# First MoE products alone, the second chunk behind them, the second tile's keys behind two weight blocks

## The chip, the core and the metric

One core of a Trainium2 chip runs the whole program. TensorE (PE) multiplies, VectorE (DVE), ScalarE (ACT) and GpSimd (POOL) compute beside it, SyncE (SP) issues most transfers. The metric is the device time of one execution in microseconds (us). TensorE's clock is granted at one of two levels, 1.2 or 2.4 GHz; the profile gives it as a share of the upper one (PEclk).

## The reference

A delta-rule attention feeds two layers of experts:

```python
k_n = k / (np.linalg.norm(k, axis=-1, keepdims=True) + 1e-06)
for t in range(S):                       # q, k, v: (4, 8, 768, 48)
    y[:, :, t] = einsum('bhd,bhde->bhe', q[:, :, t], state)
    v_old = einsum('bhde,bhd->bhe', state, k_n[:, :, t])
    state = state + beta[..., t] * outer(k_n[:, :, t], v[:, :, t] - v_old)
...
x = y as (3072 tokens, 384)
h = x @ w_in                             # 384 -> 2048
x = (h * sigmoid(1.702 * h)) @ w_out     # 2048 -> 384: "MoE 1"
p = domain_probs / (domain_probs.sum(-1, keepdims=True) + 1e-09)
out = sum over e < 4 of p[:, e] * (relu(x @ w1[e]) @ w2[e])   # 384 -> 1024 -> 384: "MoE 2"
```

## The kernel before

**Attention by chunks.** The 768 steps are cut into 12 chunks u of 64 steps; all 32 (batch, head) pairs of a chunk are computed together, in two halves of 16. Two chunks make a *tile* of 512 tokens (6 tiles). A chunk needs its keys scaled and turned (`queue_keys`, `queue_turn`: L364 load, L374 square, L377 sum, L389 to L407 inverse root by Newton steps, L420 scaling, L338 transposition, L344 copies into `kt`), Gram products of the keys (`queue_g`, L516 and L519; evicted by L524 and copies to `g`), masked products of keys and queries (`queue_q`, L447, masked by L452 into `pq`), and a triangular inverse. The first tile's inverse is VectorE's (`queue_first_inverse`): two blocks of 16 in parallel, a multiplication by beta (L626), a transposition to rows (L590), then joining products on TensorE, L656 and L665, each for both chunks. Later tiles' inverses run on GpSimd in 30 pairs of steps (`queue_inverse`, L567 and L569), begin with a transposition on VectorE (L558) and end with L573 and L590.

**The chain.** `queue_chain` carries the state SU from chunk to chunk: keys times state (L728), subtraction from v (L731), solve (L738), cross product (L748), subtraction (L753), second solve, reading of y (L761), writing of the state (L766), addition to SU (L780, L783). The copies of y go through `stage` by transfers (L842), and are split into high and low halves `xs` (`split_x`, L872), the MoE's input.

**MoE 1.** w_in and w_out are cut into 16 blocks f. A product in full precision takes three passes over high and low halves. For a block, nine products of layer 1 (L878, into `ph`) are followed by the gate on ScalarE (L979, L981), its low half `gh` on VectorE (L982), and nine products of layer 2 (L964). Layer 2 of a block stands one block later. Tile 0 runs blocks 0 to 7 on 256 columns (chunk 0) and then on the other 256 (chunk 1), blocks 8 to 15 on 512; tile 1 runs all blocks in halves (`HALVED`).

**Weight blocks.** They come as 64-bit numbers (`queue_w1`): a load (L252), scaling on ScalarE (L261), three integer instructions on VectorE (L264, L268, L272), the high half on ScalarE (L277), the low half (L280) on GpSimd or VectorE.

**The order.** All instructions of attention and weights are tasks of an `Order`: a planner with one clock per engine, a cost for each task, dependencies and a priority. It writes each engine's queue at build time; on the chip each engine works its queue in order and waits at semaphores. Between two MoE products `tick` lets it put in tasks; a task of TensorE only when `due` has run down:

```python
    def run(self, pe_ok):
        while True:
            t = self.pick(self.now, pe_ok or self.due <= 0)
            if t is None:
                return
            if t.pe:
                self.due = PE_SHARE * t.engs["PE"]
            t.issue()
```

`until(*ts)` issues tasks until those named are planned as done. Before the MoE it waits for chunk 0's y and block 0:

```python
        queue_tile(1)
        until(ydone[0], wdone[0])
```

## Time and profile before

| | us |
|---|---|
| median of 3 runs (lowest, highest) | 1516.05 (1513.36, 1517.55) |
| the profiled execution | 1515.38 |
| its span, first to last instruction | 1513.7 |
| PE busy | 1434.6 (95%) |
| DVE, ACT, POOL busy | 645.0, 460.0, 216.0 |
| mean granted clock of TensorE | 0.962 |

The attention's preparation takes the first 87 us. From there MoE 1 runs to some 700 us with attention put in, then MoE 2 to the end. "Busy" of PE is not speed: the clock column tells at which level it worked. Where PE is idle the timeline gives the gap and the engine that ended it; "issue" means that the profile shows no cause.

### The profile page before, as it was taken

What the parts mean: (1) busy time and instruction counts of PE and PEld (TensorE: products, weight loads), DVE (VectorE), ACT (ScalarE), POOL (GpSimd) and SP (SyncE); (2) the same over time, 40 slices, a digit from 0 to 9 for tenths busy, and PEclk for the clock granted to TensorE, in tenths of its full rate; (3) what the DMA queues carried; (4) which work ended last, traced back from release to release, by engine and by line L of the source; (5) the groups of instructions that cost most, each with busy time, mean ns of one, the idle gap of its engine ahead of it and who ended that gap; (6) DMA issues with size and microseconds to landing.
All of it is one profiled execution on the core that took longest, in us unless ns stands there. A gap on an engine that the chain in (4) does not pass through costs nothing.

```text
span 1513.7 us, 30460 instructions
## 1 busy us (share of the span) xinstructions
PE 1434.6 (95%) x13552; PEld 1270.2 (84%) x13552; DVE 645.0 (43%) x1076; ACT 460.0 (30%) x869; POOL 216.0 (14%) x351
## 2 busy tenths in 40 slices
PE   2689879998999999999999999999999999999998
PEld 2579669997888888887999999999999999999998
DVE  6868766647537433332223243222342223423222
ACT  5436343434334333342112131111221112212111
POOL 3214902860081170000000000000000000000000
PEclk8559979999999999999999999999999999999999
DMA  9211012012201100230000020000110000100001
GB/s 341 81 36 27 1 42 52 2 36 71 58 1 43 30 22 15 81 112 0 1 0 1 1 73 11 0 1 0 43 42 1 0 1 11 53 21 22 21 22 42
DMA packets 41333, 53.72 MB, mean 35 GB/s; under 512 B 25713, under 2 KB 29937, under 8 KB 41201
## 3 DMA queue, kind: packets, MB, share of 16 engines
q1 hardware_dynamic: 41008, 51.67, 11.1%
q8 instruction: 106, 1.74, 0.5%
q14 instruction: 27, 0.21, 0.0%
q10 hardware_dynamic: 192, 0.10, 0.0%
HBM read 42.71 MB, written 7.86 MB: 33 GB/s over the span
## 4 chain that ended last, share of the span: by engine, by line
PE 75%; DMA 1%; DVE 1%; issue 0%; SPq 0%; ACT 0%; DVEq 0%; ACTq 0%
PE ph L878 35%; PE po L1077 26%; PE px L964 8%; PE ch L738 1%; PE ch L728 1%; PE y L761 1%; PE gp L447 1%; DMA raw<-in_we_dram 1%; PE ch L766 1%; PE ch L748 1%; PE gp L516 0%; DMA stage<-scr 0%; DVE xs L872 0%; SPq L1053 0%; DVE oacc L1085 0%
## 5 line engine op out<-in xcount | busy, mean ns | idle before, releaser
L878 PE MATMUL ph<-xs,w 128*128 128x512 f32 (+1 forms) x2808 | 667.7, 381 | 3.8 <-DVE x L178 2.4
L878 PEld LDWEIGHTS ph<-xs,w 128*128 128x128 f32 x2808 | 503.0, 191 | 91.4 <-issue 2.8
L1077 PE MATMUL po<-w,hh 128*128 128x384 f32 x2304 | 432.8, 336 | 0.0
L1077 PEld LDWEIGHTS po<-w,hh 128*128 128x128 f32 x2304 | 407.6, 188 | 17.1
L1104 DVE SCALAR_TENSOR_TENSOR hh<-ph,hh 128x512 fp32r<-128x512 f32 x192 | 132.8, 692 | 555.8 <-ACT hh L1103 555.8
L1103 ACT ACTIVATE hh<-ph 128x512 fp32r<-128x512 f32 x192 | 114.8, 598 | 634.1 <-PE ph L878 634.1
L964 PE MATMUL px<-gh,w 128*128 128x512 f32 (+1 forms) x1080 | 235.9, 357 | 4.9 <-DVE gh L982 4.8
L964 PEld LDWEIGHTS px<-gh,w 128*128 128x128 f32 x1080 | 178.8, 192 | 35.6 <-DVE gh L982 7.6
L982 DVE TENSOR_TENSOR gh<-ph,gh 128x512 fp32r<-128x512 f32 (+1 forms) x120 | 69.5, 580 | 154.4 <-ACT gh L981 153.4
L979 ACT ACTIVATE ph<-ph 128x512 f32<-128x512 f32 (+1 forms) x120 | 59.5, 496 | 214.6 <-PE ph L878 211.5
L569 POOL TENSOR_TENSOR scr<-scr,itmp 128x30 f32<-128x30 f32 (+9 forms) x150 | 91.0, 607 | 11.8
L567 POOL TENSOR_TENSOR itmp<-scr 128x30 f32<-128x30 f32 (+9 forms) x150 | 82.0, 547 | 11.4
L981 ACT CAST gh<-ph 128x512 fp32r<-128x512 f32 (+1 forms) x120 | 60.1, 501 | 3.8
L738 PEld LDWEIGHTS ch<-v,scr 32*32 32x32 f32 x1536 | 41.3, 119 | 21.3 <-issue 16.2
L738 PE MATMUL ch<-v,scr 32*32 32x48 f32 x1536 | 45.7, 220 | 13.6 <-issue 10.4
L178 ACT COPY su<-ch 32x384 f32<-32x384 f32 x81 | 38.0, 470 | 52.6 <-PE ch L738 47.4
L516 PE MATMUL gp<-kt 48*32 48x64 f32 x768 | 29.9, 238 | 20.1 <-ACT kt L344 19.8
L516 PEld LDWEIGHTS gp<-kt 48*32 48x32 f32 x768 | 26.8, 121 | 23.3 <-POOL kt L344 17.9
L1069 DVE TENSOR_TENSOR xs<-x,xs 128x512 fp32r<-128x512 f32 x72 | 45.3, 683 | 2.0 <-ACT xs L1068 2.0
L1085 DVE SCALAR_TENSOR_TENSOR oacc<-po,pr,oacc 128x384 f32<-128x384 f32 x72 | 39.3, 608 | 1.3 <-PE po L1077 1.3
L1068 ACT CAST xs<-x 128x512 fp32r<-128x512 f32 x72 | 39.7, 620 | 0.0
L344 ACT COPY kt<-scr 32x512 f32<-32x512 f32 (+1 forms) x55 | 33.9, 617 | 9.2 <-DVE scr L338 8.2
(116 smaller groups left out, 850.8 us busy)
## 6 DMA issues: line engine op xcount, KB each, us to landing
raw<-in_we_dram SPq DMA_DIRECT2D x32, 384.0 KB, 3.0
rw<-in_w_dram SPq DMA_DIRECT2D x13, 768.0 KB, 11.7
k<-in_k_dram SPq DMA_DIRECT2D x12, 384.0 KB, 4.6
pq<-in_q_dram SPq DMA_DIRECT2D x24, 192.0 KB, 4.5
v<-in_v_dram SPq DMA_DIRECT2D x12, 384.0 KB, 3.0
out_dram<-oacc SPq DMA_DIRECT2D x24, 192.0 KB, 1.9
x1d<-raw SPq DMA_DIRECT2D x12, 256.0 KB, 2.2
x<-x1d SPq DMA_DIRECT2D x4, 768.0 KB, 6.6
```

Source lines behind the costliest of these rows:

```text
L516: mm(ps[r:r + SB, i, :], lhsT=kt[d:d + D, g, 0:SB], rhs=kt[d:d + D, g, :], start=True, stop=True)
L567: E.tensor_tensor(out=tv, in0=x[:, j:j + 1, j + 1:].broadcast_to([128, m, r]), in1=x[:, 0:m, j:j + 1].broadcast_to([128, m, r]), op=ALU.mult)
L569: E.tensor_tensor(out=x[:, 0:m, j + 1:], in0=x[:, 0:m, j + 1:], in1=tv, op=ALU.add)
L738: mm(cell["ps"][r:r + 32, i, :], lhsT=Tb[u][r:r + 32, g, :], rhs=V2[u][r:r + 32, g, :], start=True, stop=True, tile_position=(r, r))
L878: mm(ps, lhsT=w[:, a, kk * 128:(kk + 1) * 128], rhs=xs[kk][:, b, cs], start=kk == 0 and i == 0, stop=kk == KD - 1 and i == 2)
L964: mm(px[d][:, cs], lhsT=w[:, a, 384 + d * 128:384 + (d + 1) * 128], rhs=gh[:, b, 0:cs.stop - cs.start], start=f == 0 and i == 0 and cs.sta ...
L979: a = task(lambda: nc.scalar.activation(out=ph, in_=ph, func=AF.Gelu_apprx_sigmoid), "ACT", 0.05 + 0.43 * c, (pe,), **kw)
L981: a = task(lambda: nc.scalar.copy(out=hi, in_=ph), "ACT", 0.05 + 0.43 * c, (a,), **kw)
L982: a = task(lambda: nc.vector.tensor_tensor(out=lo, in0=ph, in1=hi.bitcast(F32), op=ALU.subtract), "DVE", 0.07 + 0.53 * c, (a,), **kw)
L1077: mm(po[b], lhsT=hh[:, a, b * 128:(b + 1) * 128], rhs=w[:, c, 384:768], start=f == 0 and i == 0, stop=f == F2 - 1 and i == 2)
L1103: nc.scalar.activation(out=hh[:, 0, :], in_=ph, func=AF.Relu)
L1104: nc.vector.scalar_tensor_tensor(out=hh[:, 1, :], in0=ph, scalar=0.0, in1=hh[:, 0, :].bitcast(F32), op0=ALU.max, op1=ALU.subtract)
```

## The change

- **MoE alone.** `until(*split)` plans chunk 0's input as ready before the MoE starts; `od.due = 7.0` keeps TensorE's tasks out for the first 7.0 us planned; `room` lets chunk 1's chain begin only after that.
- **Second chunk behind.** Its turn (L641 before), joining products and merge get a priority nine lower than the first chunk's, so each joining product is now two tasks. Its queries' products stay with the first chunk's.
- **Second tile's keys.** Priorities of chunks 2 and 3 become 12 and 13 (were 20 and 30), weight blocks 0 and 1 get 6, and the squares of chunk 2 wait for the first turn (`turns[0]`) instead of block 2. Chunk 3's square goes to a `gh` buffer.
- **First inverse.** The mask with beta before the Gram products (L482, L487) is gone: evictions multiply by a constant mask `cmask`, and beta is multiplied in after the transposition. One Newton step less for every tile.
- **Engines.** The low halves of MoE 1's weights and all key copies leave GpSimd. Block 1 no longer borrows `stage`.
- **Costs.** Some twenty planned costs are new; the second tile's inverse is planned half as long again.

```diff
-EARLY_W, LATE_W = 16, 33
+FIRST_W, EARLY_W, LATE_W = 6, 16, 33
+ALONE = 7.0
...
-        kw = dict(prio=(EARLY_W if f < N_EARLY else LATE_W) + f / 50, slack=0.5)
+        kw = dict(prio=(FIRST_W if f < 2 else EARLY_W if f < N_EARLY else LATE_W) + f / 50, slack=0.5)
...
-        wdone[f] = task(lo, ("POOL", "DVE"), (1.85, 0.95), (h,), extra=near, **kw)
+        wdone[f] = task(lo, "DVE", 0.95, (h,), **kw)
...
-        return 1 if u == 1 else 10 * u
+        return (0, 1, 12, 13)[u] if u < 4 else 10 * u
...
-            sq = task(square, "ACT", 0.75, (lk, wdone[K_AFTER] if w == 2 else None, *sqs[-1:]), prio=p,
-                      can=lambda: any_free(SCR))
+            sq = task(square, "ACT", 0.75, (lk, turns[0] if w == 2 else None, *sqs[-1:]), prio=p,
+                      can=None if u == 3 else lambda: any_free(SCR))
...
-        for fn, c in ((guess, 0.15), (newton, 0.6), (newton, 0.6), (newton, 0.6), (root, 0.6), (inverse, 0.65)):
+        for fn, c in ((guess, 0.25), (newton, 0.69), (newton, 0.69), (root, 0.69), (inverse, 0.8)):
...
-                V.tensor_tensor(out=gg, in0=cell["ps"][:, :, 0:SB], in1=gg, op=ALU.mult)
+                m = gg if w else cmask.unsqueeze(1).broadcast_to([128, 8, SB])
+                V.tensor_tensor(out=gg, in0=cell["ps"][:, :, 0:SB], in1=m, op=ALU.mult)
...
-            last = task(lambda j=j: step(j), "POOL", 0.52 + 0.0037 * m, (last,), prio=p)
+            last = task(lambda j=j: step(j), "POOL", (0.52 + 0.0037 * m) * (1.5 if w == 2 else 1.0), (last,), prio=p)
...
         def clear():
-            V.memset(X[w][:, 0:H, H:], 0.0)
+            x = cell["x"]
+            bt = BT[w].rearrange("p (h i) -> p h i", h=2)
+            V.tensor_tensor(out=x, in0=x, in1=bt.unsqueeze(2).broadcast_to([128, 2, H, H]), op=ALU.mult)
             V.memset(X[w][:, H:, 0:H], 0.0)
...
-            turned.append(task(turn, "DVE", 1.0, (last, *turned), prio=p + c, can=None if c else lambda: any_free(SCR)))
+            turned.append(task(turn, "DVE", 0.7, (last, *turned), prio=p + 9 * c, can=None if c else lambda: any_free(SCR)))
...
+        turns[w] = turned[0]
         for c, u in enumerate(us):
+            p = 1.5 + 9 * c
...
             def room(hs=hs):
+                if u == 1 and not od.moe:
+                    return None
...
         split = split_stage(*items[0])
-        od.slow = 1.0
+        until(*split)
+        od.slow, od.moe, od.due = 1.0, True, ALONE
```

Three places in TensorE's queue. In the names, `gp`, `ch` and `y` are result buffers in PSUM, `kt` keys, `pq` queries, `scr` working buffers, `v` values, `su` the state, `g` Gram blocks, `xs` the MoE's input, `w` weights; the number behind a name is the buffer's. First, from the last masked products of the first tile to its first solves, before:

```order
L447 MATMUL gp<-pq_78,kt_74 64x64 x16
L447 MATMUL gp<-pq_79,kt_75 64x64 x16
L656 MATMUL gp<-scr_97,scr_100 32x16 x128
L665 MATMUL gp<-scr_99,scr_97 32x16 x128
L738 MATMUL ch_737<-v_173,scr_99 32x48 x16
L738 MATMUL ch_760<-v_173,scr_99 32x48 x16
L748 MATMUL ch_737<-su,g 32x48 x16
L447 MATMUL gp<-pq_78,kt_74 64x64 x16
L748 MATMUL ch_760<-su,g 32x48 x16
L738 MATMUL ch_737<-v_173,scr_99 32x48 x16
L738 MATMUL ch_760<-v_173,scr_99 32x48 x16
L761 MATMUL y<-pq_78,su 48x64 x16
```

and now (the joining products are L665 and L674, the solve L747, the cross product L757):

```order
L448 MATMUL gp<-pq_78,kt_74 64x64 x16
L448 MATMUL gp<-pq_79,kt_75 64x64 x16
L665 MATMUL gp<-scr_100,scr_99 32x16 x64
L448 MATMUL gp<-pq_78,kt_74 64x64 x16
L674 MATMUL gp<-scr_98,scr_100 32x16 x64
L448 MATMUL gp<-pq_79,kt_75 64x64 x16
L747 MATMUL ch_652<-v_180,scr_98 32x48 x16
L747 MATMUL ch_673<-v_180,scr_98 32x48 x16
L757 MATMUL ch_652<-su,g 32x48 x16
L757 MATMUL ch_673<-su,g 32x48 x16
L747 MATMUL ch_652<-v_180,scr_98 32x48 x16
L747 MATMUL ch_673<-v_180,scr_98 32x48 x16
```

Half of the joining products moved out from ahead of the first solve, and two groups of masked products moved in. The other half now stands about the second y of chunk 0; behind it 32 Gram products of chunk 2 and 32 of its masked products stand ahead of the first MoE product.

Second, chunk 1's chain, which starts before the first MoE products (L878) and goes on between them:

```order
L728 MATMUL ch_984<-su,kt_75 64x48 x16
L728 MATMUL ch_1012<-su,kt_75 64x48 x16
L447 MATMUL gp<-pq_79,kt_75 64x64 x16
L878 MATMUL ph<-xs,w 128x256 x6
L738 MATMUL ch_984<-v_905,scr_99 32x48 x16
L878 MATMUL ph<-xs,w 128x256 x7
L738 MATMUL ch_1012<-v_905,scr_99 32x48 x16
L878 MATMUL ph<-xs,w 128x256 x5
L964 MATMUL px_1134<-gh,w 128x256 x2
L748 MATMUL ch_984<-su,g 32x48 x16
L964 MATMUL px_1134<-gh,w 128x256
L964 MATMUL px_1135<-gh,w 128x256 x3
```

Now its greater part stands after layer 1 of block 7, and the MoE's second half (L889, 256 columns) behind it:

```order
L757 MATMUL ch_1437<-su,g 32x48 x16
L747 MATMUL ch_1501<-v_796,scr_98 32x48 x16
L747 MATMUL ch_1437<-v_796,scr_98 32x48 x16
L757 MATMUL ch_1501<-su,g 32x48 x16
L770 MATMUL y<-pq_79,su 48x64 x16
L775 MATMUL ch_1437<-su,k_1_82 48x48 x16
L747 MATMUL ch_1501<-v_796,scr_98 32x48 x16
L770 MATMUL y<-pq_79,su 48x64 x16
L775 MATMUL ch_1501<-su,k_1_82 48x48 x16
L448 MATMUL gp<-pq_79,kt_77 64x64 x32
L889 MATMUL ph<-xs,w 128x256 x9
L977 MATMUL px_1143<-gh,w 128x256 x3
```

MoE products no longer stand between those of this chain's end; the first 72 of layer 1 stand ahead of them.

Third, the end of tile 1, where chunk 5's chain meets the first 512-wide product of tile 2 (L878), before:

```order
L748 MATMUL ch_4242<-su,g 32x48 x16
L748 MATMUL ch_4259<-su,g 32x48 x16
L738 MATMUL ch_4242<-v_4071,scr_99 32x48 x16
L738 MATMUL ch_4259<-v_4071,scr_99 32x48 x16
L761 MATMUL y<-pq_79,su 48x64 x16
L766 MATMUL ch_4242<-su,k_1_82 48x48 x16
L766 MATMUL ch_4259<-su,k_1_82 48x48 x16
L761 MATMUL y<-pq_79,su 48x64 x16
L447 MATMUL gp<-pq_78,kt_76 64x64 x32
L728 MATMUL ch_4600<-su,kt_76 64x48 x16
L728 MATMUL ch_4617<-su,kt_76 64x48 x16
L878 MATMUL ph<-xs,w 128x512 x6
```

and now (y is L770, masked products L448, layer 2 L977):

```order
L770 MATMUL y<-pq_79,su 48x64 x16
L977 MATMUL px_2850<-gh,w 128x256
L977 MATMUL px_2851<-gh,w 128x256 x3
L977 MATMUL px_2852<-gh,w 128x256 x3
L889 MATMUL ph<-xs,w 128x256 x8
L448 MATMUL gp<-pq_78,kt_76 64x64 x32
L889 MATMUL ph<-xs,w 128x256
L977 MATMUL px_2850<-gh,w 128x256 x3
L977 MATMUL px_2851<-gh,w 128x256 x3
L977 MATMUL px_2852<-gh,w 128x256 x3
L448 MATMUL gp<-pq_79,kt_77 64x64 x32
L889 MATMUL ph<-xs,w 128x512 x9
```

MoE products of tile 1 moved between the last y of chunk 5 and the first product of tile 2.

## Rows read from the trace of the kernel before

**Rows 1.** Four stretches: length, busy PE, PEld, DVE, ACT, POOL (count), PEclk, DMA, GB/s

```profile
87.40:112.70 25.30, 25.30 (x346) 22.52 (x344) 12.06 (x32) 9.21 (x22) 1.91 (x1) 0.58 0.09 32
183.00:197.00 14.00, 5.30 (x71) 4.60 (x71) 8.02 (x19) 1.41 (x3) 5.75 (x9) 0.65 0.01 1
203.00:231.00 28.00, 22.30 (x480) 19.53 (x481) 14.13 (x30) 13.55 (x30) 0.00 (x0) 0.76 0.29 78
331.00:356.00 25.00, 20.16 (x472) 18.14 (x468) 15.74 (x26) 7.98 (x17) 0.43 (x1) 0.80 0.28 71
```

**Rows 2.** Timeline of PE: start, us, engine, line, what, count, idle before and releaser

```profile
43.98 2.59 PE L656 MATMUL gp<-scr,scr 32*32 32x16 f32 x155 [11.82 <-DVE scr L641]
...
55.79 0.28 PE L738 MATMUL ch<-v,scr 32*32 32x48 f32 x1
...
73.33 1.69 PE L761 MATMUL y<-pq,su 128*48 128x64 f32 x32
...
87.39 1.65 PE L878 MATMUL ph<-xs,w 128*128 128x256 f32 x6
...
115.80 1.24 PE L964 MATMUL px<-gh,w 128*128 128x256 f32 x9
...
132.93 2.08 PE L447 MATMUL gp<-pq,kt 48*64 48x64 f32 x64
```

**Rows 3.** Timeline of DVE in the first 48 us

```profile
15.71 1.23 DVE L482 TENSOR_TENSOR scr<-gmask,bt 128x1024 f32<-128x1024 f32 x1
...
16.98 0.98 DVE L487 TENSOR_TENSOR scr<-scr,hmask 128x512 f32<-128x512 f32 x1
...
29.97 2.02 DVE L608 STREAM_TRANSPOSE scr<-scr 128x1024 f32<-128x1024 f32 x1
...
40.35 0.69 DVE L626 TENSOR_TENSOR scr<-scr,bt 128x512 f32<-128x512 f32 x1
...
44.46 2.81 DVE L452 TENSOR_TENSOR pq<-gp,pmask 64x512 f32<-64x512 f32 x4
```

**Rows 4.** Timeline of ACT before the first MoE product

```profile
76.56 2.13 ACTq L842 DMA_DIRECT2D stage<-scr  x3
...
82.12 0.41 ACT L178 CAST xs<-stage 128x256 fp32r<-128x256 f32 x1 [2.08 <-DMA stage<-scr]
```

**Rows 5.** DVE's groups by line and form, 133 to 178: busy us, mean ns, idle

```profile
L280 DVE TENSOR_TENSOR w<-rw,w 128x768 fp32r<-128x768 f32 x7 | 9.2, 1316 | 0.0
L272 DVE SCALAR_TENSOR_TENSOR rw<-rw 128x768 int32<-128x768 int32 x7 | 7.4, 1062 | 0.0
L268 DVE SCALAR_TENSOR_TENSOR rw<-rw 128x768 int32<-128x768 int32 x7 | 7.0, 1002 | 0.1
L264 DVE TENSOR_SCALAR rw<-rw 128x768 int32<-128x768 int32 x6 | 4.9, 814 | 0.0
...
L982 DVE TENSOR_TENSOR gh<-ph,gh 128x256 fp32r<-128x256 f32 x8 | 3.3, 409 | 1.1 <-ACT gh L981 1.1
```

**Rows 6.** Timeline of PE in the second and third tile's beginnings

```profile
191.83 2.77 PE L738 MATMUL ch<-v,scr 32*32 32x48 f32 x64 [8.70 <-issue]
...
210.02 1.10 PE L761 MATMUL y<-pq,su 128*48 128x64 f32 x32 [3.64 <-DVE scr L178]
...
325.14 2.07 PE L728 MATMUL ch<-su,kt 48*64 48x48 f32 x64
...
348.44 3.65 PE L728 MATMUL ch<-su,kt 48*64 48x48 f32 x64 [3.44 <-DVE pq L452]
```

**Rows 7.** Timelines of POOL and DVE around the second tile's inverse

```profile
133.53 0.16 POOL L561 MEMSET scr<- 128x32 f32 x1 [26.07 <-DVE scr L558]
...
187.46 2.03 DVE L590 STREAM_TRANSPOSE scr<-scr 128x1024 f32<-128x1024 f32 x1 [9.67 <-POOL scr L573]
```

**Rows 8.** POOL's groups by line, 133 to 189 and 254 to 332: busy, mean ns, idle

```profile
L569 POOL TENSOR_TENSOR scr<-scr,itmp 128x30 f32<-128x30 f32 (+14 forms) x30 | 26.1, 868 | 2.4
...
L569 POOL TENSOR_TENSOR scr<-scr,itmp 128x30 f32<-128x30 f32 (+14 forms) x60 | 32.5, 542 | 4.7
```

More of the change, by code (lines that the diff above doesn't have):

```diff
@@ L343, in place @@
             r, d = TR[x] + 32 * s, DR[x] + 32 * h
[L344 to L345 removed]
+            copy(e, KT[u % 4][d:d + n, :, s * 32:(s + 1) * 32], cell["t"][r:r + n, h])
         a = task(lambda: turn(0), "DVE", 0.6, deps, prio=p, can=lambda: any_free(SCR))
@@ L349, in queue_turn @@
         cell["end"] = placed[u] = tuple(
-            task(lambda e, x=x, s=s, h=h: place(e, x, s, h), ("ACT", "DVE", "POOL")[:2 + (u < 2)],
-                 (0.6, 0.42, 0.7)[:2 + (u < 2)], (b if h else a,), prio=p - 3) for h in range(2) for x in range(2) for s in range(2))
+            task(lambda e, x=x, s=s, h=h: place(e, x, s, h), ("ACT", "DVE"),
+                 (0.6, 0.42), (b if h else a,), prio=p - 3) for h in range(2) for x in range(2) for s in range(2))
         return b
@@ L369, in square @@
             def square(c=c, u=u, cell=cell):
-                sq = scr[claim(SCR, cell["end"] if c else (normed[u], normed[u + 1]))]
+                if u == 3:
+                    sq = ghp.tile([128, 2, TT], F32R, name="gh", tag="gh").rearrange("p h c -> p (h c)").bitcast(F32)
+                else:
+                    sq = scr[claim(SCR, cell["end"] if c else (normed[u], normed[u + 1]))]
                 if not c:
@@ L497, in queue_g @@
     def queue_g(u):
-        p = base(u) + 2
+        p = 8 if u in (2, 3) else base(u) + 2
         kt = KT[u % 4]
         w, c = batch[u]
-        diag, cross, halves = [], [], []
-        whole = 1 if u < 2 else 2
+        diag, cross, halves, first = [], [], [], None
+        whole = 1 if u < 4 else 2
         for g0 in range(0, NP, 8):
@@ L531, in queue_g @@
                 continue
-            a = task(lambda fs=tuple(h[1] for h in halves): [f() for f in fs], "PE", 1.51 * whole,
+            a = task(lambda fs=tuple(h[1] for h in halves): [f() for f in fs], "PE", 0.9 * whole,
                      (*placed[u], edone.get(u - 4), *diag[-1:]), prio=p, can=lambda: some_free(BANKS, whole))
+            first = first or halves[0][0]
             for hc, _, kd, kx in halves:
-                diag.append(task(kd, "DVE", 0.35, (a, premasked[w]), prio=p))
+                diag.append(task(kd, "DVE", 0.4, (a, premasked.get(w)), prio=p,
+                                 can=None if w or u or hc is not first else lambda: any_free(SCR)))
                 cross += [task(lambda e, r=r, kx=kx: kx(e, r), ("ACT", "DVE"), (0.26, 0.33), (a,), prio=p + 1)
@@ L820, in queue_chain @@
             else:
-                reads = [task(lambda: [hs[0]["read"](), *(h["write"]() for h in hs)], "PE", 2.94, (*bs, pdone[u]), prio=p,
+                reads = [task(lambda: [hs[0]["read"](), *(h["write"]() for h in hs)], "PE", 2.7, (*bs, pdone[u]), prio=p,
                               can=lambda: free_at("yg"))]
```

70 lines of the change are left out of this document (33 added, 37 removed).

## The prediction

> **What bounds the kernel now.** I read the stages first: TensorE's busy time and granted clock, stretch by stretch. From 87.4 us, where the first MoE products start, the span is TensorE's. What can be won is where it stands idle, or works at 1.2 GHz instead of 2.4. A stretch loses its idle time, plus half of the busy time at 1.2 GHz; a mean granted clock c means that a share (1 - c)/0.5 of it ran slow. Four stretches show this [rows 1]:
> - 87.4 to 112.7: never idle, but at 0.58, so 21.3 us of 25.3 slow: 10.6 lost. MoE products alternate with the small products of the second chunk's chain.
> - 183 to 197: 8.7 idle, and the 5.3 busy nearly all slow: 11.4 lost.
> - 203 to 231: 5.7 idle, 13.4 slow: 12.4 lost.
> - 331 to 356: 4.8 idle, 10.0 slow (some 1.5 of that in the idle part): 9.1 lost.
> The second view, TensorE's timeline, says who was late. At 191.83 a solve (L738) ends 8.70 us of idle time put down to nothing [rows 6]; in those us GpSimd finishes the second tile's inverse and VectorE waits 9.67 for it before turning it to rows at 187.46 [rows 7]. That inverse began at 133.53 and took 53.9 us. The addition of its steps (L569) averaged 868 ns, that of the next two inverses 542 [rows 8]. At 210.02 and 348.44 waits of 3.64 and 3.44 come at the ends of chains [rows 6].
>
> **The way to the first MoE product.** Removed from VectorE: the two masks of the first tile (1.23 + 0.98) and three short Newton instructions. Added: a multiplication as long as L626 (0.69) in place of a memset [rows 3]. GpSimd no longer places keys; ScalarE and VectorE make these four copies more. Along the queues the transposition at 29.97 comes 1.3 us earlier (between 0 and the 2.2 of the masks with the Newton instructions on top, since TensorE's first Gram products still wait for ScalarE's copies, now six instead of five). With some 0.5 added after it, the joining products start at 43.3 instead of 43.98.
>
> From there to the first solve it took 11.8 us (43.98 to 55.79) [rows 2] for 256 joining products. Now half of them (5.9) and two groups of 16 masked products stand there. 32 such products take 2.08 at 2.4 GHz, so these 32 some 4.2 at 1.2 GHz; a us of it falls into waits that are there already. I take 9.1 (8 to 10.1): solve at 52.4. From the solve to the end of the second y it was 19.2 (55.79 to 73.33 + 1.69). I keep 19: the second chunk's first join (2 us) is put in before that y, the low halves of the weights are now VectorE's (up to 1.3 each [rows 5]); in return fewer weight instructions stand between. So y ends at 71.5. The copies of y then stand behind a transposition, a low half and s_add on VectorE: transfers out at 74.5. From their issue to the input's cast it took 5.6 (76.56 to 82.12) [rows 4]: 80.1.
>
> TensorE however has Gram products and 32 products `gp<-pq,kt` of the second tile ahead of the first MoE product, and the load of their q stands behind the stage transfers on SP. I put its landing at 81.8; 2.08 x 2 after it is 85.9. First MoE product: **85.8, not 87.39**. Lower end 82.5 (input ready, q early), upper end 89.
>
> **The first half of tile 0, and the second chunk's chain.** All eight early blocks on the first 256 columns now run before the second half starts. VectorE paces them: between the gate of block 0 and the low half of block 7 stand 5 low halves, 5 + 4 + 4 weight instructions (19.1 us by the means of rows 5, an upper end: they are taken beside GpSimd's steps, which here begin only late in the stretch), and 7.6 of six gates (0.41), two masks (2.81 for four), four Gram evictions and copies (as a gate) and the transposition (2.02) [rows 3, 5]. I take 25.7 of the 26.7, from 88.9 (85.8, one cold block, 0.8 of ScalarE, the gate): block 7 can start at 114.6. The chain of chunk 1 starts at 112.6 and after block 7 lies bare: TensorE has nothing else until its y is out, moved and split. Walking it (solve, copy, cross, subtract, solve, copy, y, transfer, split) I get 23 us. Neighbours are longer: chunk 0's from solve to MoE took 31.6 at 1.2 GHz (55.79 to 87.39) [rows 2], chunk 5's from 325.14 to the MoE product behind 348.44 + 3.65 took 26.9 [rows 6]. I take 23 (20 to 29), so the second half starts at **135.5**.
>
> What is done by then: 135 half-wide MoE products and every product of chunk 1, with the Gram and `gp` products of the second tile. Before, that set plus 22 MoE products was done at 135.0 (132.93 + 2.08); nine of them take 1.24 busy [rows 2], so 22 are 2.8: 132.2. **The start loses 3.3**, though the first stretch works at 2.4 GHz: what the clock gives there, the bare chain takes. The restart after some 4 us of waiting for the transfer is slow too: 2.3 more.
>
> **The second tile.** Its keys are squared right after the first turn and its inverse starts with the transposition that stands before the fifth gate, at about 104.5 instead of 133.5. 53.9 us later, 158.4. TensorE comes to the products that need it at 135.5 + 27 (the blocks in between) + 2.3 = 164.8. Before it had 49.6 us (133.5 to 183.1) and needed 58.3; now it has 60. So **11.4 come back**. Chunks 2 and 3 then run between 512-wide products of tile 0 (five blocks left, not the last two), so the bare stretch 203 to 231 goes: **12.4**. At the third tile's beginning the last y stands some 7 us of work ahead of the first 512-wide product; copies, transfer and split need about 6.5: **9.1 come back**, barely.
>
> Not free: blocks 8 to 15 still pace VectorE (1.0 lost against TensorE). Chains put between MoE products by estimated times will wait here and there; bounds are nothing and the 5.7 + 4.8 idle of the two old stretches; I take half, 5.5.
>
> **Sum.** 11.4 + 12.4 + 9.1 = 32.9, less 3.3, 2.3, 1.0 and 5.5: 20.8. The span of 1513.7 becomes 1492.9, with the 1.7 outside it 1494.6; that execution is 0.67 below the median of three. **Forecast 1495 us.**
>
> **A rule against it.** GpSimd's additions took 1.6 times as long in the first inverse as in the next two [rows 8]; beside the first one VectorE split weights, 1.32 us for a low half [rows 5]. The Trainium skill (Advanced Engine Details and Errata, GPSIMD Details) says that the Pool engine shares a read and a write interface with VectorE, in conflict with VectorE instructions of two SBUF inputs. By that rule the new order, with more two-input work on VectorE, would stretch the inverse further. This is rival B.
>
> **Rivals.**
> A. The start wins as well: q lands early (first product 83), the bare chain takes 20, and half of my 5.5 + 1.0 isn't lost: 9 better, 1486. For it: every estimate above is walked along full queues.
> B. The inverse ends last again. VectorE has no idle stretch beside it; a fifth longer makes 53.9 into 64.7, ending at 169.2, rows at 171.2, against 164.8: 6.4 of waiting and 2.6 of slow restart: 1504. Against it: 6 us of slack and the bare chain, in which VectorE rests.
> C. The change doesn't do what it says: the holes of 203 to 231 and 331 to 356 move to other chains. Then 32.9 shrinks to 11.4 and the sum is near zero: 1516.
> D. Slower. Each of the first eight blocks waits for its own weights, and VectorE, in order, in turn waits for TensorE and ScalarE (gates and Gram evictions stand between weight instructions). Price: one round trip per block. From 2.6 us a block on, eight of them eat the 20.8; at 3.4 us, 27 go: 1522. For it: on VectorE gates and weights alternate. Against it: my walk finds some 1 to 3 us in two or three blocks only.
>
> **Chances.** Forecast 0.52, A 0.20, B 0.13, C 0.07, D 0.08. About 0.3% (4.5 us) is what a measurement can tell from no change: faster 0.86 (forecast, A, B and a little of C), same 0.06, slower 0.08. The forecast's own range is 1487 to 1503; with A and B, 1481 to 1508.
>
> **What would show it.** Right: first MoE product near 86, granted clock 1.0 soon after it; TensorE idle or on small products alone for some 10 us before 135; no wait at the second tile's first solve; rows of that inverse near 160; no idle time over 1 us between 160 and 260. Wrong: MoE products waiting for VectorE's low halves in most of the first blocks (D); a wait on the inverse at 165 (B); waits over 3 us at the chains of chunks 3 and 5 (C).

## The result, and the profile after

The changed kernel takes 1498.14 us (median; 1497.07 to 1501.52), the kernel before 1515.6 beside it. The ratio is 0.9889, 95% interval 0.9868 to 0.991: 1.1% faster. The profiled execution has a span of 1496.2 us, where before had 1513.7. The prediction was 1495 (1481 to 1508), faster: sign and range hold, and the centre is 3 us too low. The start loses 5 us more than the sum had, and the later stretches give back what it had. The parts of the change do not add up the way its sum does, as the experiments show.

The same stretches as [rows 1], now of the changed kernel, with the bare chain and the wait behind it as two more (columns as there: length, busy PE, PEld, DVE, ACT, POOL, granted clock, DMA share, GB/s):

```profile
87.40:112.70 25.30, 19.96 (x307) 18.04 (x307) 20.97 (x30) 13.74 (x29) 7.71 (x14) 0.86 0.01 2
112.70:132.00 19.30, 15.97 (x394) 14.35 (x390) 18.89 (x24) 8.71 (x20) 17.81 (x20) 0.82 0.08 23
132.00:145.00 13.00, 7.55 (x80) 7.28 (x81) 12.82 (x15) 4.82 (x9) 12.02 (x13) 0.63 0.34 69
183.00:197.00 14.00, 14.00 (x345) 11.60 (x340) 8.82 (x17) 9.90 (x22) 0.00 (x0) 1.00 0.12 35
203.00:231.00 28.00, 27.01 (x571) 23.61 (x565) 16.97 (x31) 12.69 (x29) 0.00 (x0) 1.00 0.24 72
331.00:356.00 25.00, 23.12 (x420) 19.41 (x416) 19.21 (x40) 11.09 (x21) 0.00 (x0) 1.00 0.30 86
```

The three later stretches are as predicted: busy and at full clock, where before stood idle or at half clock. The first is not. With MoE products alone the granted clock is higher (0.58 before, 0.86 now), but TensorE is idle for 5.3 of 25.3 us there, and for 5.5 of the 13 us from 132 to 145. TensorE's timeline of the changed kernel names the waits (start, us, what, count, idle before and what ended it):

```profile
79.46 3.67 PE L448 MATMUL gp<-pq,kt 48*64 48x64 f32 x62 [0.87 <-DMA pq<-in_q_dram]
...
105.06 1.86 PE L889 MATMUL ph<-xs,w 128*128 128x256 f32 x7 [2.34 <-DVE w L280]
...
112.23 1.14 PE L737 MATMUL ch<-su,kt 48*64 48x48 f32 x32 [0.33 <-DVE pq L453]
...
129.95 1.52 PE L775 MATMUL ch<-su,k 64*48 64x48 f32 x32
136.53 0.44 PE L448 MATMUL gp<-pq,kt 48*64 48x64 f32 x2 [5.06 <-DMA pq<-in_q_dram]
137.89 3.67 PE L448 MATMUL gp<-pq,kt 48*64 48x64 f32 x62 [0.91 <-DMA pq<-in_q_dram]
141.49 2.29 PE L889 MATMUL ph<-xs,w 128*128 128x256 f32 x9
...
170.47 2.07 PE L737 MATMUL ch<-su,kt 48*64 48x48 f32 x64
```

Single blocks wait for VectorE's low halves (L280; 4.2 us in three waits). Chunk 1's chain starts at 112.23; its last product ends at 131.5, and the next MoE product comes at 141.49. Between these two TensorE waits for the q of chunk 3 (5.06 and 0.91), and its clock is near half (0.53 from 135 to 140, 0.50 from 140 to 145). What a stretch loses (its length less busy time times granted clock, added up over windows of 5 us), in us:

| stretch | before | after | predicted difference | measured |
|---|---|---|---|---|
| 60 to 145 | 28.2 | 38.8 | +5.6 (3.3 + 2.3) | +10.6 |
| 145 to 360 | 38.0 | 10.9 | -26.4 (32.9 less 1.0 and 5.5) | -27.1 |

The two rows together are 16.5 less; the spans differ by 17.5. From 360 on the loss falls by another 2, which the prediction did not have. What 0 to 60 adds can't be told, since the clock reads 1.00 up to 25 or 30 us there whatever the products take (last section), so the sum is not closed to the last us or two.

### The profile page after: what moved, and what is told of

Same layout as the page of the kernel before. It is cut to its first block, busy times and chain, and to the rows that moved or that the text cites. A ratio compares the mean times of both kernels' runs of the same rounds, so it can differ in the third digit from the quotient of the medians.

```text
span 1496.2 us, 30416 instructions
## 1 busy us (share of the span) xinstructions
PE 1427.9 (95%) x13552; PEld 1264.9 (85%) x13552; DVE 648.5 (43%) x1074; ACT 458.9 (31%) x864; POOL 200.1 (13%) x341
## 4 chain that ended last, share of the span: by engine, by line
PE 90%; DVE 4%; DMA 2%; issue 1%; ACT 1%; SPq 1%; POOL 1%; DVEq 0%; POOLq 0%; ACTq 0%
PE ph L889 40%; PE po L1091 27%; PE px L977 13%; PE ch L747 2%; PE y L770 2%; PE gp L448 2%; DMA pq<-in_q_dram 2%; PE ch L737 1%; PE ch L775 1%; PE ch L757 1%; PE gp L515 1%; DMA rw<-in_w_dram 1%; SPq L853 1%; DVE pq L453 0%; DVE gh L995 0%
## 5 line engine op out<-in xcount | busy, mean ns | idle before, releaser
L889 PE MATMUL ph<-xs,w 128*128 128x512 f32 (+1 forms) x2808 | 666.7, 380 | 8.2 <-DVE w L280 4.2
L889 PEld LDWEIGHTS ph<-xs,w 128*128 128x128 f32 x2808 | 502.0, 191 | 95.7 <-DVE w L280 4.8
L977 PE MATMUL px<-gh,w 128*128 128x512 f32 (+1 forms) x1080 | 233.9, 356 | 2.3 <-DVE gh L995 2.2
L977 PEld LDWEIGHTS px<-gh,w 128*128 128x128 f32 x1080 | 179.5, 194 | 31.0 <-DVE gh L995 3.8
L571 POOL TENSOR_TENSOR itmp<-scr 128x30 f32<-128x30 f32 (+9 forms) x150 | 84.7, 565 | 11.4
L180 ACT COPY su<-ch 32x384 f32<-32x384 f32 x73 | 34.4, 471 | 55.2 <-PE ch L747 47.5
L515 PE MATMUL gp<-kt 48*32 48x64 f32 x768 | 29.3, 233 | 20.1 <-ACT kt L180 19.8
L448 PE MATMUL gp<-pq,kt 48*64 48x64 f32 x768 | 34.1, 255 | 11.4 <-DMA pq<-in_q_dram 10.2
L747 PEld LDWEIGHTS ch<-v,scr 32*32 32x32 f32 x1536 | 36.5, 110 | 9.1 <-issue 4.6
L448 PEld LDWEIGHTS gp<-pq,kt 48*64 48x64 f32 x768 | 31.4, 167 | 14.6 <-issue 10.5
L565 POOL MEMSET scr<- 128x32 f32 x5 | 0.8, 159 | 311.7 <-DVE scr L562 311.7
L747 PE MATMUL ch<-v,scr 32*32 32x48 f32 x1536 | 40.4, 208 | 2.1 <-DVE v L762 1.9
```

Of the source, the lines that this page charges most:

```text
L448: mm(ps[TR[x]:TR[x] + C, i, :], lhsT=kt[d:d + D, g, :], rhs=pq[d:d + D, g, x, :], start=True, stop=True)
L515: mm(ps[r:r + SB, i, :], lhsT=kt[d:d + D, g, 0:SB], rhs=kt[d:d + D, g, :], start=True, stop=True)
L571: E.tensor_tensor(out=tv, in0=x[:, j:j + 1, j + 1:].broadcast_to([128, m, r]), in1=x[:, 0:m, j:j + 1].broadcast_to([128, m, r]), op=ALU.mult)
L747: mm(cell["ps"][r:r + 32, i, :], lhsT=Tb[u][r:r + 32, g, :], rhs=V2[u][r:r + 32, g, :], start=True, stop=True, tile_position=(r, r))
L889: mm(ps, lhsT=w[:, a, kk * 128:(kk + 1) * 128], rhs=xs[kk][:, b, cs], start=kk == 0 and i == 0, stop=kk == KD - 1 and i == 2)
L977: mm(px[d][:, cs], lhsT=w[:, a, 384 + d * 128:384 + (d + 1) * 128], rhs=gh[:, b, 0:cs.stop - cs.start], start=f == 0 and i == 0 and cs.sta ...
```

## Experiments

The small diffs are against the changed kernel unless another is named. Chunks 0 and 1 make the first tile, 2 and 3 the second, 4 and 5 the third. "Q" is short for a chunk's masked products `gp<-pq,kt` (L448).

**1. Is it the wait for q at 136 and 232?** The planner takes a load of q to land 2.5 us after issue; in the trace of the changed kernel it lands after 4.5 us in the median (at least 3.7), and the load stands behind the transfers of y on SyncE's queue.

```
-        lq = task(load, "HW", 1.28, (edone.get(u - 2), normed[u]), lat=2.5, prio=p, slack=5)
+        lq = task(load, "HW", 1.28, (edone.get(u - 2), normed[u]), lat=2.5 if u < 3 else 5.0, prio=p, slack=5)
```

> One number changed in the changed kernel: from chunk 3 on the order is planned as if the load of q (pq) landed 5.0 us after its issue, not 2.5. The masked products gp<-pq,kt of chunk 3 then stand behind one block of MoE products of the second half, those of chunk 4 likewise later; chunk 2's stay. Theory 1 (the waits of 5.06 + 0.91 us at 136 us and of 2.29 + 1.04 us at 232 us, and the slow products behind them, cost the span what they last): the second half starts when its input is split, at 138.4 instead of 141.5 (3.1), the 32 masked products run inside warm work (1.6 of their 3.67), and the hole at 232 goes (3.3 + 1.6): 9.6 faster, some 1488 us. Rival (VectorE's weights pace blocks 8 to 15, and the input is what is late at 136): at most the 3 us at 138 come, or they return as waits for weights: 1495 to 1498.

Measured: 1498.58 us, ratio 0.9904 (0.9886 to 0.9922): no gain. The rival holds, as TensorE's and VectorE's rows of this kernel show:

```profile
134.52 0.58 PE L889 MATMUL ph<-xs,w 128*128 128x256 f32 x1 [3.29 <-ACT xs L180]
139.22 2.28 PE L889 MATMUL ph<-xs,w 128*128 128x256 f32 x8 [4.11 <-DVE xs L883]
141.42 3.68 PE L448 MATMUL gp<-pq,kt 48*64 48x64 f32 x64
```

```profile
137.39 0.96 DVE L264 TENSOR_SCALAR rw<-rw 128x768 int32<-128x768 int32 x1
138.26 2.38 DVE L883 TENSOR_TENSOR xs<-stage,xs 128x256 fp32r<-128x256 f32 x3
```

With Q out of the way TensorE waits for the input's split (L883) instead, which stands on VectorE behind weight instructions and ends at 140.6. In the changed kernel it ends at 140.75 as well. Two things were equally late, and taking one away shows the other. The waits for q at 232 did go (175 to 240 loses 1.2 us, where the changed kernel loses 5.9), and the time still did not move; experiment 7 comes back to this.

**2. The same for every chunk.**

```
-        lq = task(load, ..., lat=2.5, ...)
+        lq = task(load, ..., lat=5.0, ...)
```

> The same number for every chunk: also chunk 2's masked products leave their place in front of the first MoE product, and stand behind chunk 1's chain; by the order, chunk 1's chain then stands between MoE products earlier, and is not bare at its end. Theory 1 (the wait for q sets the start of the first MoE product): the first MoE product at 79 instead of 83.1, and the second half starts with more done ahead of it: 4 to 8 us below the kernel with chunks 3 and 4 alone, 1480 to 1485 us. Rival (the first eight blocks are paced by VectorE's weights, which come no earlier): the four us return as waits of MoE products for the low halves (4.2 us now, then 8), and the time is that of the kernel with chunks 3 and 4 alone.

Measured: 1484.58 us, 0.981 (0.979 to 0.983), 14 us below the changed kernel. The time is as Theory 1 had it, but the 6.0 us by which the first MoE product comes earlier (77.08, not 83.06) are the smaller part: 80 to 145 loses 10.6 us instead of 26.9. Chunk 1's chain begins at 88 and stands between MoE products (TensorE's rows, this kernel):

```profile
88.15 1.14 PE L737 MATMUL ch<-su,kt 48*64 48x48 f32 x32 [1.08 <-ACT g L180]
89.22 1.33 PE L889 MATMUL ph<-xs,w 128*128 128x256 f32 x9
```

**3. Only chunk 2's q, and chunks 2 and 3.** (`lat=5.0 if u == 2 else 2.5`, and `lat=5.0 if u < 4 else 2.5`.)

> Only chunk 2's load of q is planned to land 5.0 us after its issue; chunks 3 and later keep 2.5. With all chunks at 5.0 the time was 1484.6, with chunks 3 and later alone 1498.6. Theory 1 (it is chunk 2's masked products in front of the first MoE product, and the place of chunk 1's chain that hangs on them): 1482 to 1487 us; chunk 3's masked products again wait for their load, at most 3 us. Rival (the gain needs chunks 3 and 4 as well, since their waits take it back): 1489 to 1494 us.

> Chunks 2 and 3 at 5.0 us, later chunks at 2.5 as in the changed kernel. With all chunks at 5.0, chunk 5's masked products came so late that TensorE waited 3.39 us for their masks at 314 us and worked at 1.2 GHz to 327 behind it (9.9 us lost in 300 to 330). Theory 1 (that hole is due to the late masked products of chunk 5 and goes with them): 1475 to 1480 us. Rival (a hole at the end of that chain stands in any order, as in the kernel before at 348): 1483 to 1487 us.

Measured: 1488.53 (0.9836; 0.9815 to 0.9856) and 1490.65 (0.985; 0.983 to 0.9871). Chunk 2's Q alone brings 9.6 of the 14 us, which lies between the two expectations (up to 1487, and from 1489). The second run refutes its Theory 1, and it lies above its rival (1483 to 1487) as well. The hole at 300 to 330 stands in all three kernels (10.0 to 10.7 us lost), and it was never chunk 5's Q that stood there. The loads of q go out in the order of the chunks; the one that TensorE waits for here, issued at 319.12, is chunk 7's, and the masks it waits for with every q later are chunk 6's. Rows of TensorE, SyncE and VectorE of the first of the two:

```profile
323.41 0.44 PE L448 MATMUL gp<-pq,kt 48*64 48x64 f32 x2 [6.55 <-DMA pq<-in_q_dram]
324.56 3.68 PE L448 MATMUL gp<-pq,kt 48*64 48x64 f32 x62 [0.70 <-DMA pq<-in_q_dram]
328.17 3.01 PE L889 MATMUL ph<-xs,w 128*128 128x512 f32 x9
```

```profile
314.79 4.23 SPq L853 DMA_DIRECT2D stage<-scr  x6
319.12 1.28 SPq L434 DMA_DIRECT2D pq<-in_q_dram  x2
```

```profile
321.36 1.89 DVE L883 TENSOR_TENSOR xs<-stage,xs 128x512 fp32r<-128x512 f32 x3
```

The third tile's first MoE product (328.17) needs chunk 5's y, which leaves only at 314.79 and is split at 323.25. It starts 4.9 us after that, because chunk 7's Q stands ahead of it in TensorE's queue and waits for a load behind the six transfers of y. Chunk 2's Q has the same place ahead of the first MoE product of all.

**4. The two large parts undone, one at a time and together.** First the stretch of MoE products alone:

```
-        self.moe = False
+        self.moe = True
...
-        until(*split)
-        od.slow, od.moe, od.due = 1.0, True, ALONE
+        od.slow = 1.0
```

> The changed kernel with the MoE products not alone at the start: chunk 1's chain may begin before the first MoE product and stands between the half-wide products, as in the kernel before; the second tile's keys stay early. Theory 1 (alone loses: what the clock gives from 85 to 110 us, the bare chain from 113 to 141 takes): the granted clock of 85 to 110 falls from 0.8 to about 0.6, but no bare chain follows and the masked products of chunk 3 wait for nothing; the second half starts 6 to 9 us earlier, some 1489 to 1492 us. Rival (alone pays, as the change has it): the stretch of 25 us at 0.6 costs 10 us, and the chain is paid all the same: 1505 us.

Then the second tile's keys:

```
-        return (0, 1, 12, 13)[u] if u < 4 else 10 * u
+        return 1 if u == 1 else 10 * u
...
-        p = 8 if u in (2, 3) else base(u) + 2
+        p = base(u) + 2
...
-            sq = task(square, "ACT", 0.75, (lk, turns[0] if w == 2 else None, *sqs[-1:]), prio=p,
+            sq = task(square, "ACT", 0.75, (lk, wdone[2] if w == 2 else None, *sqs[-1:]), prio=p,
```

> The changed kernel with the second tile's keys where they were: squares behind weight block 2, Gram products and inverse at their old priority; MoE products alone at the start stay. Theory 1 (the early inverse is what wins): the inverse starts near 130 and ends near 180, TensorE waits 7 to 9 us at the second tile's first solve and runs slow behind it, and chunks 2 and 3 are bare again: 11.4 + 12.4 come back as loss, 1515 to 1522 us. Rival (the other parts win: start, placement at the halves): the inverse is late again, but it costs less than half of that: 1500 to 1508 us.

And both:

> The changed kernel with both large parts undone: the second tile's keys late, and no stretch of MoE products alone; masks, joining products, priorities of the weights and planned costs stay as changed. With one of the two parts undone the time hardly moved (1497.1 and 1499.7). Theory 1 (the two parts stand in for each other: each alone wins some 14 us, and together they spoil the start, where chunk 1's chain is bare): with both undone the time is that of the kernel before, 1510 to 1518 us. Rival (neither part is what wins, the small edits are): 1495 to 1502 us.

Measured: 1497.09 without MoE alone (0.9908; 0.988 to 0.9935), 1499.71 with late keys (0.9916; 0.989 to 0.9943), 1504.65 with both undone (0.9944; 0.9926 to 0.9963). The seven runs without MoE alone spread from 1494 to 1507 us, and the profiled one took 1506.3; the median lies between its two expectations. Each part by itself brings 5 to 8 us over "both undone" (4 to 6 by the ratios), and the two together 6.5 (8.3 by the ratios). That is not the sum of the two; how much more than one part it is can't be told, as the intervals overlap. My theory for the late keys (1515 to 1522) fell, and its rival (1500 to 1508) is nearer. The hole did return, as three windows of that kernel show,

```profile
175.00:190.00 15.00, 12.77 (x322) 11.27 (x324) 10.14 (x16) 7.04 (x15) 6.25 (x11) 0.80 0.01 3
190.00:205.00 15.00, 13.62 (x316) 12.99 (x316) 6.74 (x11) 4.39 (x10) 12.88 (x29) 0.52 0.10 28
205.00:220.00 15.00, 11.93 (x236) 10.61 (x231) 8.91 (x16) 5.40 (x12) 13.28 (x23) 0.71 0.28 63
```

and 175 to 240 loses 20.6 us where the changed kernel loses 5.9. But with the keys out of the way chunk 1's chain stood between MoE products, and 80 to 145 lost 7.8 us instead of 26.9. The both-undone theory is half right (1510 to 1518 expected): what stays changed in that kernel (masks, the second chunk put off, engines, priorities of the weights, planned costs) brings some 9 us of its own. Which of it does was not tested, except for the second chunk's join.

**5. The second chunk's join not put off.**

```
-            ... prio=p + 9 * c, can=None if c else lambda: any_free(SCR)))
+            ... prio=p + c, can=None if c else lambda: any_free(SCR)))
...
-            p = 1.5 + 9 * c
+            p = base(us[-1]) + c
```

> The changed kernel with the second chunk's joining products not put off: they stand directly behind the first chunk's, in front of its first solve, as before. By the order chunk 1's chain then begins after two blocks of MoE products and stands between them. Theory 1 (the bare chain of chunk 1 costs more than the earlier start brings): the first MoE product comes some 4 us later, near 87, but no stretch before the second half is without MoE products, 8 to 13 us back there: 1488 to 1492 us. Rival (the early start is worth its 4 us, and the chain is paid either way): 1500 to 1503 us.

Measured: 1491.45 us, 0.9853 (0.9829 to 0.9877), as Theory 1 had it. The first MoE product came at 84.2, hardly later, and 80 to 145 lost 16.0. Together with the rest of the change this edit cost 7 us by the times, 5 by the ratios.

**6. Why chunk 1's chain is late.** Chunk 2's Q (79.46, above) fills two of the three PSUM banks that the chain uses too, and its masks (L453) stand behind weights on VectorE. VectorE's rows of the changed kernel:

```profile
110.79 1.39 DVE L453 TENSOR_TENSOR pq<-gp,pmask 64x512 f32<-64x512 f32 x2
112.10 0.41 DVE L995 TENSOR_TENSOR gh<-ph,gh 128x256 fp32r<-128x256 f32 x1
112.46 0.97 DVE L280 TENSOR_TENSOR w<-rw,w 128x768 fp32r<-128x768 f32 x1
113.41 0.55 DVE L740 TENSOR_TENSOR v<-v,ch 128x384 f32<-128x384 f32 x1
114.00 1.39 DVE L453 TENSOR_TENSOR pq<-gp,pmask 64x512 f32<-64x512 f32 x2
```

The chain's first product, at 112.23, was released by the first two of these masks. The experiment moves one priority:

```
-                    c.setdefault("end", []).append(task(f, "DVE", 0.6, (t,), prio=p + 1))
+                    c.setdefault("end", []).append(task(f, "DVE", 0.6, (t,), prio=7 if u == 2 else p + 1))
```

> The changed kernel with one priority moved: VectorE's masks of chunk 2's products gp<-pq,kt come ahead of the weights (7 instead of 26). The products keep their place in front of the first MoE product, and their load its planned 2.5 us. In the changed kernel these products take two of the three PSUM banks that the chain also uses (yg, ch0, ch1), and their masks are done only at 110.8 to 115.4 us, behind weights; chunk 1's chain gets its bank at 112.2. Theory 1 (the bank held by waiting masks sets chunk 1's chain): the chain starts some 15 to 20 us earlier, stands between MoE products, and 10 to 15 us come back before 145 us; chunk 5's end then waits as in the other kernels with an early chain (10 lost between 300 and 360): 1486 to 1492 us. Rival (it is the products' place in front, or their load, that costs): the first MoE product stays near 83, and the time at 1496 to 1500 us.

Measured: 1498.64 us, 0.9911 (0.9887 to 0.9935). The mechanism is as Theory 1 says; the time is as the rival had it. The first MoE product came at 83.64, as in the changed kernel, and the chain already at 87.52 (TensorE's rows):

```profile
83.64 3.95 PE L889 MATMUL ph<-xs,w 128*128 128x256 f32 x18
87.52 1.14 PE L737 MATMUL ch<-su,kt 48*64 48x48 f32 x32
```

80 to 145 lost 14.5 instead of 26.9: 12.4 us back. All of it was given back later, 2.4 between 145 and 300 and 9.9 between 300 and 360.

**7. Where it is given back.** In most of these kernels the span behind the third tile's first MoE product is nearly the same, 1160 to 1162 us. The table has the start of GpSimd's inverse for the second and the third tile (L565, before L561), the start of the third tile's first product, and the span left from there, in us. The trace without MoE alone is that of an execution of 1506.3 us, 9 above the median.

| kernel | second tile's inverse | third tile's | first product of third tile | rest of span |
|---|---|---|---|---|
| before | 133.5 | 254.6 | 352.0 | 1161.7 |
| after | 104.0 | 231.5 | 335.6 | 1160.6 |
| masks first (6) | 108.3 | 233.8 | 337.3 | 1161.6 |
| q of 3 and 4 on later (1) | 103.9 | 234.6 | 333.6 | 1162.0 |
| no MoE alone (4) | 111.2 | 239.0 | 343.1 | 1161.5 |
| chunk 2's q later (3) | 98.9 | 223.9 | 328.2 | 1160.0 |
| q of 2 and 3 later (3) | 96.4 | 221.0 | 328.8 | 1161.6 |
| join not put off (5) | 88.7 | 225.1 | 327.9 | 1161.5 |
| every q later (2) | 96.0 | 220.8 | 318.0 | 1164.0 |
| keys late (4) | 128.9 | 189.9 | 330.5 | 1166.0 |
| both undone (4) | 135.8 | 193.1 | 335.1 | 1170.6 |

Down to "every q later" the first product follows the third tile's inverse by 97 to 108 us, and that inverse follows the second tile's by 121 to 136. It looks as if one path set the time: inverse, chains of chunks 2 and 3, Gram products, inverse, chains of chunks 4 and 5. In the changed kernel the end of that path and TensorE's own work come together, as its one short wait there shows:

```profile
336.88 2.11 PE L889 MATMUL ph<-xs,w 128*128 128x512 f32 x8 [0.78 <-DVE xs L883]
```

So less loss in front of this place brings nothing as long as chunk 5's y comes no earlier (experiments 1 and 6). In the last two kernels the third tile's keys come ahead of chunk 2's chain; the inverses stand close together there, and the product comes at 330.5 and 335.1 all the same.

That the inverses themselves are late on the chip is not shown, and two things in the traces speak against it. First, in the changed kernel the third tile's inverse ends at 271.32, and VectorE turns it to rows only at 280.89 (L594). It stands idle for 5.2 us in between, waiting for three gates that are ahead in its queue. So the planner's order, and not GpSimd, sets when the rows are ready. Second, "q of 2 and 3 later" and "every q later" have the same inverses to 0.4 us, and their first products are 10.8 us apart. In the former, chunk 7's Q stands in front of the product. It does so in "masks first", "no MoE alone", "chunk 2's q later" and "join not put off" too. In these five TensorE first waits 6.0 to 7.0 us for that q, and the product starts 4.6 to 6.4 us after its input is split. In "masks first" the split was done at 330.92:

```profile
332.27 0.45 PE L448 MATMUL gp<-pq,kt 48*64 48x64 f32 x2 [6.96 <-DMA pq<-in_q_dram]
...
337.27 3.46 PE L889 MATMUL ph<-xs,w 128*128 128x512 f32 x9
```

With every q later the product starts when the split ends (317.97 and 317.93). So of what the earlier chains give back, at most some 5 us (6.4 in "masks first") belong to chunk 7's Q, and the rest to the wait for chunk 5's y. Which planned cost sets the place of chunk 5's chain stays open, and masks first together with a later q for chunk 7 was not run.

Two runs bear on the waits at this place. The third tile's first eight blocks can be taken by halves, so that work that needs chunk 4 alone stands in front of the wait (on top of experiment 2):

```
-HALVED = {0: N_EARLY, 1: 16}
+HALVED = {0: N_EARLY, 1: 16, 2: 8}
```

> The kernel with every chunk's q planned 5.0 us after its issue (1484.6 us), and with the first eight blocks of the third tile (chunks 4 and 5) also taken by halves of 256 columns. In that kernel 9.9 us are lost between 300 and 330, around the place where the third tile's first 512-wide product waits for chunk 5's y. Theory 1 (the chains and inverses, which start no earlier than before, now set the end of chunk 5; MoE products that need chunk 4 alone can stand in front): the first half's 8 blocks, some 17 us of work, cover the wait, 1474 to 1478 us. Rival (the halves cost as much as they cover, or the wait moves to the second half): 1483 to 1487 us.

Measured: 1479.41 us, 0.977 (0.9749 to 0.9792), the fastest complete kernel of this study and 2.3% faster than before. TensorE is never idle from 300 to 360:

```profile
300.00:330.00 30.00, 30.00 (x589) 28.54 (x588) 18.67 (x36) 14.04 (x34) 1.91 (x1) 1.00 0.31 86
330.00:360.00 30.00, 30.00 (x589) 28.54 (x588) 23.14 (x53) 16.24 (x39) 0.00 (x0) 1.00 0.15 32
```

The 10.0 us lost there are gone; 5.2 arrive in the time, between the two expectations (to 1478, and from 1483). And the same with q loaded from ScalarE's queue:

```
-                nc.sync.dma_start(out=pq[DR[x]:DR[x] + D, :, x, :], in_=q[u, x])
+                (nc.sync if u < 2 else nc.scalar).dma_start(out=pq[DR[x]:DR[x] + D, :, x, :], in_=q[u, x])
...
-        lq = task(load, "HW", 1.28, (edone.get(u - 2), normed[u]), lat=5.0, prio=p, slack=5)
+        lq = task(load, "HW" if u < 2 else "ACT", 1.28, (edone.get(u - 2), normed[u]), lat=4.0, prio=p, slack=5 if u < 2 else 0.5)
```

> The same halves, and q is loaded from ScalarE's queue instead of SyncE's from chunk 2 on, planned 4.0 us after its issue. On SyncE's queue the load stands behind six transfers of y to the stage, which took 4.2 us to issue at 315 us in one of the runs. Theory 1 (that queue is what makes q late): no wait for pq over 1 us, and 0 to 4 us below the kernel with halves alone. Rival (ScalarE issues in order, and gates and copies of y stand behind the load): waits for gates or copies instead, 2 to 6 us above the kernel with halves alone.

Measured: 1482.54 us (1479.41 to 1486.16), 0.9796 (0.9773 to 0.9819). No wait for q is left in the trace from 60 us on, but none was left with halves alone either. The time is 3.1 us above that of halves alone, as the rival had it (2 to 6), and five of its six runs lie above all of those. The intervals of the ratios overlap, and the profiled execution is the one that is as fast as halves alone, so where the others lose is not seen.

**8. What sets the inverse's pace.** On top of experiment 2, three of four VectorE operations on the weights of blocks 8 to 15 are left out, so the values there are not the weights:

```
-                cell["t"], cell["top"] = cell["lo"].bitcast(F32), cell["hi"].bitcast(F32)
+                cell["t"], cell["top"] = cell["lo" if f < N_EARLY else "hi"].bitcast(F32), cell["hi"].bitcast(F32)
...
-            b = task(low, "DVE", 0.6, (dep, begun[0]), **kw)
-            c = task(shift, "DVE", 0.88, (a, b), **kw)
-            dep = task(sign, "DVE", 0.88, (c,), **kw)
+            b = task(low, "DVE", 0.6, (dep, begun[0]), **kw) if f < N_EARLY else a
+            c = task(shift, "DVE", 0.88, (a, b), **kw) if f < N_EARLY else a
+            dep = task(sign, "DVE", 0.88, (c,), **kw) if f < N_EARLY else a
```

> The kernel with every chunk's q planned at 5.0 us, and three of the four VectorE operations on the weights of blocks 8 to 15 left out, so that their values are not the weights. It measures what VectorE's weight work does to GpSimd's inverse beside it: that inverse took 58.2 us in the changed kernel and 53.9 before, the later ones some 38. Theory 1 (VectorE's weight work beside it slows GpSimd): 38 to 46 us, additions of the steps under 650 ns, and with the earlier inverses the hole at 300 to 330 goes: below 1475 us. Rival (GpSimd's pace does not depend on VectorE): 54 us or more, and the hole stays.

Measured: 1477.16 us (two runs; 0.9755; 0.972 to 0.9791), where Theory 1 had below 1475. The third tile's first product comes at 312.3, without the hole. That is no proof for the inverses' path, because the order moved too: the third tile's inverse starts at 170.65 here, ahead of chunk 3's chain, and at 220.81 in experiment 2. What the run does show is the pace. GpSimd's first and last step of the second tile's inverse, here, and then in the kernel of experiment 2:

```profile
97.49 0.16 POOL L565 MEMSET scr<- 128x32 f32 x1 [87.16 <-DVE scr L562]
...
141.44 1.92 POOL L577 TENSOR_TENSOR scr<-scr,bt 128x1024 f32<-128x1024 f32 x1
```

```profile
95.96 0.15 POOL L565 MEMSET scr<- 128x32 f32 x1 [85.62 <-DVE scr L562]
...
152.65 1.92 POOL L577 TENSOR_TENSOR scr<-scr,bt 128x1024 f32<-128x1024 f32 x1
```

45.9 us instead of 58.6, with no other work on GpSimd. VectorE's three weight operations with two inputs (L268, L272, L280) take 12.4 us beside this inverse, and 34.3 beside that of experiment 2. For the pace Theory 1 holds, at the upper end of its 38 to 46; the additions average 713 ns (946 in experiment 2), above the 650 expected. The third tile's inverse of the changed kernel takes 39.8 us; what keeps this one above that is not shown.

## The prediction, step by step

| step | predicted | measured |
|---|---|---|
| joining products | 43.3 | 40.9 |
| first solve | 52.4 | 51.3 |
| second y ends | 71.5 | 70.0 |
| first MoE product | 85.8 | 83.1 |
| chunk 1's chain starts | 112.6 | 112.2 |
| block 7 starts | 114.6 | 113.3 |
| second half starts | 135.5 | 141.5 |
| inverse begins, ends | 104.5, 158.4 | 104.0, 162.2 |
| TensorE needs the inverse | 164.8 | 174.7 |

- **The way to the first MoE product** was 2.7 us long in sum, and 2.4 of that is there at the joining products. The transposition of 29.97 comes at 26.52, so 3.4 us earlier; the prediction took 1.3, with 2.2 as its bound. From joining products to first solve it was 10.4, just past the 8 to 10.1 given. That Q with its late load stands ahead of the product was seen; what else that placement does was not (below).
- **The first half of tile 0**: block 7 starts within 1.3 us of the forecast, though the first product came 2.7 us earlier, so the stretch is 1.4 longer. The clock is not 1.0 all the way: it reads 0.72 from 95 to 100 and 0.70 from 105 to 110, after waits for low halves of 1.21 and 2.34. Such waits in three blocks (4.2 us) are what the prediction granted rival D.
- **The bare chain, 23 us**, is the term that was mis-sized: 112.2 to 141.5 is 29.3, the far end of the 20 to 29 given. The prediction had some 4 us of waiting at its end, which puts the last product's end at 131.5, and so it was. The wait is 10.0 us instead. The split stands behind weight instructions on VectorE, and takes 2.37 us there, beside GpSimd's steps, where it took 1.15 before they began (VectorE's rows; the last section has a case where it takes 1.08 beside them):

```profile
78.19 1.15 DVE L883 TENSOR_TENSOR xs<-stage,xs 128x256 fp32r<-128x256 f32 x3
...
138.38 2.37 DVE L883 TENSOR_TENSOR xs<-stage,xs 128x256 fp32r<-128x256 f32 x3
```

  Chunk 3's Q, with its load behind the transfers, was missing in the walk and ends at nearly the same time (141.5, the split at 140.75).
- **Why the chain is bare at all** was not asked. The prediction read its place from the order and did not ask what held it there: a bank, full of chunk 2's Q, whose masks had a low priority (experiment 6).
- **The second tile.** 53.9 us for the inverse became 58.2. VectorE turns it to rows at 168.87, 6.7 us after its end and not near 160 as forecast. TensorE first needs them at 174.7, 9.9 us later than predicted; 6.0 of these are the second half's late start. Rival B did not come, and in part that is luck: the slower inverse met a later need. The 11.4 of 183 to 197 came back.
- **The rule named in the prediction** (the Trainium skill, Advanced Engine Details and Errata, GPSIMD Details) pointed the right way. The inverse went from 53.9 to 58.2 us with more two-input work on VectorE beside it (the three weight operations take 27.1 us there before, 34.6 now), and from 58.6 to 45.9 with less (experiment 8).
- **203 to 231 and 331 to 356**: back, as predicted. A smaller hole of 3.3 us idle opens at 230 (waits for q of 2.29 and 1.04). It is inside the 5.5 set aside for new waits, but the sign "no idle time over 1 us between 160 and 260" fails by it.
- **Why it is faster**: the prediction gave the gain to three holes one by one, and by stretches that sum comes out (27.1 us back, 26.4 forecast). But the holes are not three separate gains. The third tile's first product comes 16.4 us earlier than before, the span behind it is the same to 1.1 us, and what is saved in front counts only as far as that product moves (experiments 1, 6 and 7). That late keys lose little (experiment 4) was not foreseen: another order of chains and Gram products gets there as well.

## What to carry over

A wait removed on the busiest engine is worth something only up to the next path that ends at the same place: before summing holes, follow the second-longest path (here the chains up to chunk 5's y) to the point where both meet, and see how far apart they are. Then look at what stands directly in front of that point in the queue (here chunk 7's Q). Work placed early for filling holds its buffers until the last reader is done; give that reader a priority as early as the work's, or what shares the buffers is what waits. When two late things end together, undoing one of them shows no gain and is no evidence that it was harmless.
